# Fixing the issue order by hand in a recurrent-attention and feed-forward kernel

## The chip, the cores and the metric

The kernel runs on one core of a Trainium2 chip. The metric is the device time of one execution in microseconds (us). Before the change three runs had a median of 198.59 us (197.66 to 199.28). The profile adds one traced execution of each kernel; its span, from the first to the last instruction, was 195.0 us before. The profiled run itself was timed at 196.82 us, so a timed figure is about 2 us above a span.

The engines are called by the profile's names: PE is the tensor engine (PEld its weight loads), DVE is VectorE, ACT is ScalarE, POOL is GpSimd and SP issues most DMAs. Each engine has its own stream of instructions.

## The reference, cut to what matters

```python
# B, H, S, D = 4, 8, 768, 48
for t in range(S):
    state = alpha[:, :, t, :, None] * state + einsum('bhd,bhde...', k_t, v_t)   # outer product
    y[:, :, t] = einsum('bhd,bhde->bhe', q_t, state)
x = y.transpose(0, 2, 1, 3).reshape(3072, 384)
h = maximum(maximum(x @ w1, x @ w2), x @ w3)      # 384 -> 768
return (h @ w_out).astype(float32)                # 768 -> 384
```

The kernel cuts the sequence into blocks of 128 positions and takes two batches together. That gives 12 *steps* (6 blocks x 2 pairs of batches). A step goes through these pieces:

- **decays** (`N`, `D`): logarithm of alpha, cumulative sums by a triangular product, two exponentials; then q and k are scaled (the "q product" and the "k product"), and v by a constant (`V`);
- **turn** (`T`): q and k are transposed on PE, DVE copies them to `qkT`;
- **scores** (`A`): eight products per batch on 48 rows each, of heads at rows 0 to 47 and heads at rows 64 to 111, then a mask on DVE;
- **attention** (`Y`) and **turn back** (`X`), which gives `xT`;
- **state** (`S`): the state for the next block;
- **gates** (`G0` to `G8`): x against w1, w2, w3. Three groups of products per third of the weights; ACT copies two of them, DVE takes two maxima and writes `hT`;
- **output** (`O`): `hT` against `w_out`, an ACT copy and a store.

A gate group is 6 products of 256 columns; a step has 9 groups.

## The kernel before

The scheduler of the programming layer decides each engine's order. The kernel gives it whole stages:

```python
def cast_weights():                       # the casts are shared by three engines
    for e, dst, src in wstage:
        (nc.scalar.copy, nc.vector.tensor_copy, nc.gpsimd.tensor_copy)[e](out=dst, in_=src)   # shortened

# stage_a, per batch u: decays
lps = ps.tile([P, 512], FP32, name="lps", tag="w", bufs=2)
...
nc.gpsimd.tensor_mul(kv, rk[:, hs], ic)
nc.vector.tensor_mul(qv, rq[:, hs], ac)
...
nc.gpsimd.tensor_scalar_mul(vt, raws.pop((s, "v")), vs_c)

# stage_b: turn, scores, attention, turn back
for p in range(HP):
    for i in range(2):
        rows = slice(64 * i, 64 * i + D)
        nc.tensor.matmul(aps[i][:, p, :], qkT[rows, u, 1, p, :], qkT[rows, u, 0, p, :], ...)
...
nc.scalar.copy(out=xT..., in_=xtp)

# ffn, per third of the weights
nc.scalar.copy(out=h0, in_=gs[0])
nc.scalar.copy(out=h1, in_=gs[1])
nc.vector.tensor_max(h0, h0, h1)          # two fp16 inputs in SBUF
nc.vector.tensor_max(hs, gs[2], h0)

load(1); load_weights(); load(2); load(3)      # after load(0)
stage_a(0); stage_b(0); stage_a(1); cast_weights()       # shortened
for s in range(NS):
    load(s + 4); stage_b(s + 1); stage_a(s + 2); stage_c(s); ffn(s)     # with bounds
```

The kernel keeps eight buffers in PSUM, which holds PE's results, in three rings (a ring is a set of buffers used in turn): the ring `w` (2 buffers: decays, turns, scores), the ring `s` (2: attention, turn back, state, output) and the ring `g` (4: gates).

## Time and profile before

| what | value | view |
|---|---|---|
| span | 195.0 us | page |
| PE busy in 0:10, 40:50, 130:140 | 1.64, 7.02, 9.98 us | table by stretches |
| mean length of five late steps | 13.95 us, (168.68 - 98.93) / 5 | output products in the timeline |
| one gate group, late | 0.66 us | chain of waits |
| first gate products | 23.3 us | timeline |

The table by stretches gives, for each window, the busy time and the instruction count of each engine, the clock granted to PE, and the mean share and rate of the DMA engines. (PEclk is 1.00 also where the trace has no record of the clock: here the first record lies at 27.3 us, so the first two windows say nothing on it.) These are four windows of the kernel before:

```profile
core 0: us, PE busy (x) PEld busy (x) DVE busy (x) ACT busy (x) POOL busy (x), PEclk, DMA share, GB/s
0.00:10.00 10.00, 1.64 (x17) 1.31 (x18) 2.98 (x10) 4.25 (x8) 2.17 (x6) 1.00 1.05 186
10.00:20.00 10.00, 7.33 (x68) 4.88 (x66) 5.45 (x8) 5.44 (x11) 4.46 (x4) 1.00 1.28 256
40.00:50.00 10.00, 7.02 (x57) 4.46 (x55) 4.88 (x10) 4.93 (x12) 4.55 (x5) 0.83 1.19 213
130.00:140.00 10.00, 9.98 (x122) 7.52 (x120) 6.18 (x11) 6.74 (x15) 4.83 (x5) 1.00 1.00 197
```

PE starts slowly, has a hole in 40:50, and is busy almost all of the time late on. The timeline (start, duration, engine, line, operation, names, shapes, count) of a late step shows how the scheduler mixed half-row scores (line 193) into the gates (line 252):

```profile
158.32 0.49 PE L252 MATMUL gps_2615<-xT,wcat 128*128 128x256 f16 x3
158.83 0.39 PE L193 MATMUL aps_2504<-qkT 48*128 48x128 f16 x4
...
159.21 0.49 PE L252 MATMUL gps_2615<-xT,wcat 128*128 128x256 f16 x3
159.63 0.40 PE L193 MATMUL aps_2505<-qkT 48*128 48x128 f16 x4
```

The scores come four at a time, all four on the same rows, with full-height products (those that use all 128 rows of PE's array) between one four and the next. The duration of a group includes the pipeline's end, so starts are what to count with: 3 gate products from 158.32 take 3 x 0.109 = 0.33 us, to 158.65, and the scores only start at 158.83.

### The profile page before, as it was taken

The page shows a single profiled execution, that of the slowest core. Times are in us where ns is not written, and L with a number is a line of the kernel's source. Part 1 is how long each engine was busy: PE and PEld are TensorE (multiplying, and loading weights), DVE is VectorE, ACT ScalarE, POOL GpSimd, SP SyncE. Part 2 cuts the span into 40 slices and gives each one's busy share as a digit, 9 for nine tenths or more (in the row PEclk, how much of TensorE's full clock was granted, in tenths as well). Part 3 has the DMA queues.
Part 4 walks back from the last instruction along what each step waited for, and adds up shares of the span by engine and source line. Part 5 has one row for each costly group of instructions (what it writes and reads, how often), then busy time and mean ns, then how long its engine had stood idle before and what let it go on. Part 6 is the DMA issues. An engine that isn't in the chain of part 4 may idle for free.

```text
span 195.0 us, 4340 instructions
## 1 busy us (share of the span) xinstructions
PE 167.9 (86%) x1736; PEld 122.5 (63%) x1736; DVE 116.8 (60%) x200; ACT 110.7 (57%) x221; POOL 61.2 (31%) x64
## 2 busy tenths in 40 slices
PE   0295886958869979999989999999989999999992
PEld 0164564845556857766767857857757767778680
DVE  3272845526746996448468568667477666765250
ACT  2518066682552946753954956847827639446551
POOL 0443722054180646800540631703922304100000
PEclk9999999996999988999999999999999999999999
DMA  7999999999996059379699909819720020020102
GB/s 147 223 218 284 351 357 224 225 198 228 239 190 135 0 147 228 78 158 202 167 232 217 194 29 221 166 68 225 116 75 9 3 81 3 0 81 3 74 9 81
DMA packets 107252, 28.69 MB, mean 147 GB/s; under 512 B 99808, under 2 KB 107232, under 8 KB 107232
## 3 DMA queue, kind: packets, MB, share of 16 engines
q1 hardware_dynamic: 106944, 28.32, 67.5%
q8 instruction: 13, 0.21, 0.5%
q10 hardware_dynamic: 288, 0.10, 0.2%
q14 instruction: 7, 0.06, 0.1%
HBM read 23.69 MB, written 4.72 MB: 146 GB/s over the span
## 4 chain that ended last, share of the span: by engine, by line
PE 41%; DVE 16%; ACT 13%; issue 9%; POOL 9%; DMA 5%; SPq 4%; POOLq 0%; DVEq 0%; ACTq 0%
PE ops L267 7%; DVE hT L263 5%; PE tps L179 5%; ACT ic L157 4%; DMA rq<-in_q_dram 3%; SPq L85 3%; DMA ra<-in_alpha_dram 2%; ACT xb L208 2%; POOL vt L167 2%; POOL qk_86 L163 2%; ACT ac L158 2%; PE yps L204 2%; POOL gt L221 1%; DVE qkT L182 1%; PE xtp L210 1%
## 5 line engine op out<-in xcount | busy, mean ns | idle before, releaser
L252 PEld LDWEIGHTS <-wcat 128*128 128x128 f16 x648 | 58.0, 98 | 12.2 <-ACT wcat L131 1.9
L267 PE MATMUL ops<-wo_97,hT 128*128 128x384 f16 x144 | 29.2, 342 | 6.1 <-DVE hT L263 2.9
L167 POOL TENSOR_SCALAR vt<-rv,c_69 128x768 f16<-128x768 f32 x12 | 27.2, 2267 | 1.8 <-DMA rv<-in_v_dram 1.8
L267 PEld LDWEIGHTS <-hT 128*128 128x128 f16 x144 | 13.5, 102 | 18.2 <-DVE hT L263 7.6
L182 DVE COPY qkT<-tps 128x1024 f16<-128x1024 f16 x24 | 15.6, 686 | 14.9 <-PE tps L179 14.9
L208 ACT ACTIVATE xb<-yps,c_69 128x384 f16<-128x384 f32 x24 | 14.0, 583 | 17.7 <-PE yps L204 17.4
L270 ACT COPY ob<-ops 128x384 f32<-128x384 f32 x24 | 11.1, 488 | 20.2 <-PE ops L267 18.0
L193 PEld LDWEIGHTS <-qkT 48*128 48x128 f16 x192 | 11.7, 100 | 9.8 <-DVE qkT L182 4.3
L204 PE MATMUL yps<-vt,lat 128*128 128x48 f16 x192 | 14.9, 189 | 0.5 <-DVE lat L196 0.2
L163 POOL TENSOR_TENSOR qk_86<-rk,ic 128x384 f16<-128x384 f32 x6 | 6.0, 997 | 28.6 <-ACT ic L157 28.6
L157 ACT ACTIVATE ic<-lps,c_69 128x384 f32<-128x384 f32 x24 | 14.0, 584 | 1.3 <-PE lps L151 1.1
L163 POOL TENSOR_TENSOR qk_87<-rk,ic 128x384 f16<-128x384 f32 x6 | 6.0, 997 | 26.6 <-ACT ic L157 26.6
L158 ACT ACTIVATE ac<-lps,c_69 128x384 f32<-128x384 f32 x24 | 14.0, 584 | 0.0
L204 PEld LDWEIGHTS <-lat 128*128 128x128 f16 x192 | 11.5, 100 | 3.3 <-DVE lat L196 1.9
L163 POOL TENSOR_TENSOR qk_84<-rk,ic 128x384 f16<-128x384 f32 x6 | 6.2, 1039 | 21.2 <-ACT ic L157 21.2
L163 POOL TENSOR_TENSOR qk_85<-rk,ic 128x384 f16<-128x384 f32 x6 | 6.3, 1042 | 17.3 <-ACT ic L157 17.3
L211 ACT COPY xT<-xtp 128x768 f16<-128x768 f16 x12 | 9.6, 797 | 0.6 <-PE xtp L210 0.4
L210 PE MATMUL xtp<-c_68,xb 128*128 128x128 f16 x72 | 8.8, 236 | 1.0 <-ACT ge L159 0.5
L164 DVE TENSOR_TENSOR qk_84<-rq,ac 128x384 f16<-128x384 f32 x6 | 4.8, 808 | 7.5 <-DMA rq<-in_q_dram 6.0
L201 PEld LDWEIGHTS <-qkT 128*128 128x128 f16 x80 | 7.6, 97 | 0.7
L210 PEld LDWEIGHTS <-xb 128*128 128x128 f16 x72 | 4.5, 103 | 5.7 <-ACT xb L208 5.4
L164 DVE TENSOR_TENSOR qk_85<-rq,ac 128x384 f16<-128x384 f32 x6 | 4.6, 766 | 4.9 <-ACT ac L158 4.9
(436 smaller groups left out, 372.4 us busy)
## 6 DMA issues: line engine op xcount, KB each, us to landing
ra<-in_alpha_dram SPq DMA_DIRECT2D x12, 384.0 KB, 4.9
rk<-in_k_dram SPq DMA_DIRECT2D x12, 384.0 KB, 6.2
rq<-in_q_dram SPq DMA_DIRECT2D x12, 384.0 KB, 5.7
rv<-in_v_dram SPq DMA_DIRECT2D x12, 384.0 KB, 5.5
out_dram<-ob SPq DMA_DIRECT2D x24, 192.0 KB, 2.0
ws_0_106<-in_moe_w_dram SPq DMA_DIRECT2D x1, 384.0 KB, 5.1
ws_1_108<-in_moe_w_dram SPq DMA_DIRECT2D x1, 384.0 KB, 4.5
ws_2_110<-in_moe_w_dram SPq DMA_DIRECT2D x1, 384.0 KB, 5.1
```

Of the source, the lines that this page charges most:

```text
L157: nc.scalar.activation(out=ic, in_=lv, func=AFT.Exp, bias=nat_c, scale=-1.0)
L158: nc.scalar.activation(out=ac, in_=lv, func=AFT.Exp, bias=at_c, scale=1.0)
L163: nc.gpsimd.tensor_mul(kv, rk[:, hs], ic)
L167: nc.gpsimd.tensor_scalar_mul(vt, raws.pop((s, "v")), vs_c)
L182: nc.vector.tensor_copy(out=qkT[:, u], in_=tps)
L193: nc.tensor.matmul(aps[i][:, p, :], qkT[rows, u, 1, p, :], qkT[rows, u, 0, p, :], start=True, stop=True)
L204: nc.tensor.matmul(yps[:, p, i, :], la_[:, i, p, :], vt[:, u * H + 2 * p + i, :], start=(cb == 0), stop=(cb == 0 or i == 1))
L208: nc.scalar.mul(xb, yps.rearrange("p a b d -> p (a b d)"), ys_c)
L210: nc.tensor.transpose(xtp[:, u, f, :], xb[:, f * P:(f + 1) * P], ident)
L252: nc.tensor.matmul(gps[:, j, :], wcat[:, f, g, jj * P:(jj + 1) * P], xT[:, f].rearrange("p u t -> p (u t)"), start=(f == 0), stop=(f == NF ...
L267: nc.tensor.matmul(ops, hT[:, jj, u * P:(u + 1) * P], wo16[:, jj, :], start=(jj == 0), stop=(jj == NJ - 1))
L270: nc.scalar.copy(out=ob, in_=ops)
```

## The change

Its intent: take the order out of the scheduler's hands, do the attention of three steps before the first gates so that the wait for weights is filled, let each arriving third of the weights serve two steps, and keep PE's clock up early with products whose result is not used. Work also moves between engines. The core of the diff (helper functions that only became separate pieces are cut):

```diff
-    def cast_weights():                     # three engines
+    def cast_weights(_, i):
+        for dst, src in wstage[3 * i:3 * i + 3]:
+            nc.gpsimd.tensor_copy(out=dst, in_=src)
 ...
-            nc.gpsimd.tensor_mul(kv, rk[:, hs], ic)
-            nc.vector.tensor_mul(qv, rq[:, hs], ac)
+        eng = nc.vector if s < 3 else nc.gpsimd
+        nc.gpsimd.tensor_mul(kv, raws[s, "k"][:, hs], ic)
+        eng.tensor_mul(qv, raws[s, "q"][:, hs], ac)
 ...
-        nc.gpsimd.tensor_scalar_mul(vt, raws.pop((s, "v")), vs_c)
+        nc.scalar.mul(vt, raws.pop((s, "v")), vs_c)
 ...
-        nc.scalar.copy(out=xT.rearrange("p f u t -> p u f t"), in_=xtp)
+            nc.vector.tensor_copy(out=xT.rearrange("p f u t -> p u f t"), in_=xtp_of.pop(s))
 ...
+    def warm(_, n):
+        wps = ps.tile([P, 512], FP32, name="wps", tag="g", bufs=4)
+        for _ in range(n):
+            nc.tensor.matmul(wps, blank[:, :P], blank, start=True, stop=True)
 ...
+    # letter = piece, digit = batch, gate group or count, @n = step; without @ the loop's step plus an offset
+    PROLOGUE = """N0@0 H11@0 D0@0 D1@0 N0@1 H8@0 V0@0 T0@0 T1@0 A0@0 A1@0 D0@1 Y0@0 D1@1 X0@0 Y1@0
+        T0@1 H2@0 A0@1 T1@1 N0@2 V0@1 A1@1 X1@0 Y0@1 D0@2 D1@2 X0@1 H5@0 T0@2 Y1@1 M0@0 T1@2
+        S0@0 V0@2 A0@2 S1@0 W0 X1@1 A1@2 W1 W2 W3"""
+    FIRST = """G0@0 G1@0 G2@0 G0@1 G1@1 G2@1 Y0@2 G3@0 G4@0 G5@0 G3@1 G4@1 Y1@2 X0@2 G5@1 G6@0 G7@0
+        G8@0 G6@1 X1@2 G7@1 G8@1"""
+    SECOND = """N0@3 G0 G1 G2 D0@3 D1@3 M0@1 G3 G4 O0@0 G5 T0 O1@0 G6 N0 S0 O0@1 A0 V0@3 G7 T1 D0 S1
+        O1@1 A1 G8 Y0 Y1 D1 M0 X0 V0 X1"""
+    STEADY = """T0 S0 N0 G0 G1 D0 T1 S1 O1 A0 G2 G3 O0 A1 G4 Y0 G5 Y1 X0 G6 D1 X1 G7 V0 G8 M0"""
+    LAST = """G0 G1 G2 G3 G4 G5 O0 G6 G7 G8 O1"""
     load(1)
+    load(2)
     load_weights()
-    load(2)
     load(3)
+    load(4)
 ...
+    with tc.manual_schedule():
+        emit(0, PROLOGUE); emit(0, FIRST)                   # joined here
+        for s in range(2, NS):
+            emit(s, {2: SECOND, NS - 1: LAST}.get(s, STEADY))
```

`M` computes the state's gates; `T`, `A`, `Y`, `X` without `@` mean the next step, `N`, `D`, `V` the one after it, `O` and `S` the one before.

## The prediction

> **What bounds the kernel now.** The profiled span is 195.0 us (timed median 198.59). The table by stretches shows three regimes.
>
> - 0 to 30 us is start-up: the tensor engine is busy 1.6, 7.3 and 8.9 of each 10 us, and products run at half speed: 16 transposes took 1.90 us (0.89 later), six gate products 1.29 us (0.66 later). Full speed comes at 34 us.
> - 30 to 80 us has holes: busy 7.0 in 40:50, 8.0 in 50:60. At 44.4 us, after 2.6 us idle, twelve output products took 3.7 us instead of 1.98.
> - From 80 us the tensor engine is busy 9.4 to 10 of 10 us (one dip, 8.8); a step takes 13.6 to 14.4 us (output products at 142.2, 156.6, 170.2 us in the chain of waits).
>
> Start-to-start times of a late step, from the timeline: gates 54 x 0.1094 = 5.91, output 1.98, transposes in 0.90, scores 16 x 0.082 = 1.31, attention 0.70, transposes back 0.36, decays 0.54, state 0.66: 12.36 us. So about 1.2 us a step are short waits (hT, qkT, xb) and switches.
>
> **What changes.** Product counts stay, but for 26 idle products early (off the path). On ACT, xT copies (0.80) leave and v scaling comes (estimate 0.85): 9.9 us per step. Vector loses q products from step 3 and gains xT: 9.3. GpSimd loses the 2.2 us v scaling and gains two 1.0 us products: 4.6. None reaches 12.3. All casts go to GpSimd: 12 x 0.83 us, and weights land every 1.15 us.
>
> Step 2's loads move ahead of the weights: 1.57 MB at the measured 0.22 MB/us delays weights by 7.1 us, to 25.6 us for the first, groups complete about 28, 31.6, 35.8, output 39. The three attention steps end near 26 us, so this wait is filled, and two steps per group (3.9 us of products against 3.5 us of loading) make the tensor engine the limit.
>
> **Sum.** Gates of step 0 start about 26.5 us. The first two steps' gates (FIRST) are 12.9 us of products, plus 2 us for landings and slow products: 41.5. SECOND: 14.9 us, ends 56.5. Eight steady steps at 12.3: 155. LAST and output 9.9, then copy and store (3.3 us at the chain's end): 168.
>
> One gain is hard to size: scores now alternate rows 0 and 64. The Trainium skill, "TensorE: Matmul & The Clock Gate", Part 3, says weight loads overlap running products only where row groups differ; before, four on the same rows came every 82 ns. If they pair, 0.3 to 0.7 us a step. Against it I set 0.4 us of waits a step, since a fixed order cannot slip past a late operand. Net span 167, timed 170.
>
> **What would show it right.** First gate products at 25 to 28 us; FIRST done by 40 to 43; no tensor idle over 1.5 us and no slow output products (310 ns) after 45 us; steady period 12.0 to 12.7, busy over 9.5 in every stretch; scores closer than 82 ns; weights landing 7 us later, with no loss.
>
> **What would make it wrong.** Two PSUM buffers per ring, or ACT's order (80% busy), stalling every steady step: each 0.3 us costs 3 us. The tensor engine going slow between 20 and 30 us (the same page, Part 1, says some 3.4 us of idleness halve the clock; this trace agrees after start and at 44 us). Scores pairing fully: 4 us better. Step 3's loads, now last, landing at 46 us while SECOND wants its transposes at 47.
>
> Time 170 us, range 164 to 177. Chances: faster by over 2% 0.97, within 2% 0.02, slower 0.01.

## The result, and the profile after

The changed kernel took 176.37 us (median of four runs, one of them slow) against 198.67 us for the kernel before. The ratio is 0.8873, with a 95% interval of 0.8824 to 0.8923. Here and below, a ratio is the mean time of one kernel's fast runs over the mean of the other's fast runs of the same rounds, so it is not quite the ratio of the quoted medians. The profiled span is 174.4 us.

The four windows, for the kernel after:

```profile
core 0: us, PE busy (x) PEld busy (x) DVE busy (x) ACT busy (x) POOL busy (x), PEclk, DMA share, GB/s
0.00:10.00 10.00, 7.95 (x38) 3.31 (x39) 3.22 (x11) 4.20 (x7) 2.16 (x6) 1.00 1.03 182
10.00:20.00 10.00, 6.26 (x74) 4.02 (x72) 6.69 (x10) 5.32 (x10) 1.99 (x2) 0.68 1.38 219
...
40.00:50.00 10.00, 9.92 (x96) 8.38 (x95) 4.82 (x10) 7.67 (x16) 4.15 (x5) 1.00 0.93 180
...
130.00:140.00 10.00, 9.22 (x123) 7.68 (x122) 7.04 (x12) 8.27 (x16) 3.07 (x5) 1.00 0.08 27
```

The hole in 40:50 is closed. In 130:140, though, PE is busy *less* than before (9.22 against 9.98) and still gets more done, because a step needs fewer busy microseconds. Four steady steps measured from one output to the next each show 12.04 us of PE busy time in 12.82 us; the five late steps before had 67.09 us of busy time in 69.75, so 13.42 in 13.95 each.

The scores explain most of that (f2 below). In the timeline of the kernel after (tiles `aps_872` are on rows 0 to 47, `aps_873` on rows 64 to 111):

```profile
52.14 1.14 PE L282 MATMUL ops<-wo_97,hT 128*128 128x384 f16 x6
53.21 0.23 PE L193 MATMUL aps_872<-qkT 48*128 48x128 f16 x1
53.21 0.23 PE L193 MATMUL aps_873<-qkT 48*128 48x128 f16 x1
53.27 0.22 PE L193 MATMUL aps_872<-qkT 48*128 48x128 f16 x1
53.28 0.22 PE L193 MATMUL aps_873<-qkT 48*128 48x128 f16 x1
```

Two scores start within 0.01 us of each other, and the next pair 0.06 us later. The page "TensorE: Matmul & The Clock Gate" of the Trainium skill describes this in Part 3: products on different row groups run at the same time in the array. This trace agrees, in that the starts differ by 0.01 us or less.

Where the 20.6 us of the span came from, by milestones in the two timelines:

| milestone | before | after | gain so far |
|---|---|---|---|
| first output product of step 2 | 74.9 | 63.0 | 11.9 |
| first output product of step 9 | 168.7 | 152.4 | 16.3 |
| first output product of step 11 | 189.2 | 168.7 | 20.5 |

The milestones have not done quite the same work: the new order is further ahead with attention, which is why its last step has only gates and outputs left and gains another 4 us there. (The 168.7 is the start of the seventh of the last 18 output products, which begin at 167.76 us; the first six belong to step 10.)

What did *not* go to plan is visible too. The gates start at 31.34 us, and the granted clock was 0.68 in 10:20. And every steady step has one hole on PE. The timelines of DVE, POOL and PE around it, in this order:

```profile
97.93 1.27 DVE L275 TENSOR_TENSOR h_1698<-h_1698,h_1730 128x512 f16<-128x512 f16 x1 [1.03 <-ACT h_1730 L273]
99.30 0.69 DVE L276 TENSOR_TENSOR hT<-gps_1734,h_1698 128x512 f16<-128x512 f32 x1
99.91 0.68 DVE L183 COPY qkT<-tps 128x1024 f16<-128x1024 f16 x1
```

```profile
96.95 1.00 POOL L159 TENSOR_TENSOR qk_87<-rk,ic 128x384 f16<-128x384 f32 x1 [6.84 <-ACT ic L155]
97.91 1.01 POOL L160 TENSOR_TENSOR qk_87<-rq,ac 128x384 f16<-128x384 f32 x1
```

```profile
97.45 0.61 PE L179 MATMUL tps<-c_68,qk_87 128*128 128x128 f16 x8
...
99.54 0.33 PE L146 MATMUL lps<-la_80,c_68 128*128 128x384 f16 x1
100.64 0.61 PE L179 MATMUL tps<-c_68,qk_87 128*128 128x128 f16 x8 [0.78 <-DVE qkT L183]
```

The maximum at line 275 takes 0.42 us elsewhere in the same step (at 104.13 and at 107.08 us). Here it takes 1.27 us, beside POOL's q product at 97.91 us, which the change had moved to POOL. The page "SBUF — State Buffer" of the Trainium skill, section "Who interferes with whom", says that a DVE instruction with two SBUF inputs contends with a GpSimd instruction that reads SBUF, and that one of them blocks. The trace fits: POOL's q product runs until 98.92 us and the maximum ends 0.28 us after it. It is not any POOL instruction, though: in the kernel before, the maximum at 98.66 us took 0.41 us in the middle of POOL's scaling of v (from 97.67 us), and of the eleven maxima and q products that ran on DVE wholly beside that scaling nine took their usual time. So the change took a neighbour off POOL that mostly did not disturb DVE, and put one there that does. The copy to `qkT` stands behind the maximum in DVE's order, the ring `w` has only two buffers, and so the second turn waits 0.78 us.

### The profile page after: what moved, and what is told of

Its sections match the earlier page's. It is cut to its first block, busy times and chain, and to the rows that moved or that the text cites. A ratio compares the mean times of both kernels' runs of the same rounds, so it can differ in the third digit from the quotient of the medians.

```text
span 174.4 us, 4372 instructions
## 1 busy us (share of the span) xinstructions
PE 156.9 (90%) x1762; PEld 120.2 (69%) x1762; DVE 116.1 (67%) x191; ACT 108.4 (62%) x205; POOL 57.1 (33%) x78
## 4 chain that ended last, share of the span: by engine, by line
PE 78%; DVE 10%; ACT 4%; DMA 3%; issue 2%; SPq 1%; ACTq 0%; DVEq 0%
PE ops L282 14%; PE tps L179 6%; DVE qkT L183 4%; DVE lat L196 4%; DMA rq<-in_q_dram 3%; PE yps L210 2%; PE lps L146 2%; PE xtp L222 2%; PE yps L207 2%; PE wps L293 2%; PE sps L250 2%; PE sps L247 1%; SPq L85 1%; ACT xb L214 1%; PE lps L149 1%
## 5 line engine op out<-in xcount | busy, mean ns | idle before, releaser
L268 PEld LDWEIGHTS <-wcat 128*128 128x128 f16 x648 | 59.8, 98 | 8.7 <-issue 0.3
L282 PE MATMUL ops<-wo_97,hT 128*128 128x384 f16 x144 | 27.0, 326 | 0.6 <-DVE st_1_93 L254 0.6
L282 PEld LDWEIGHTS <-hT 128*128 128x128 f16 x144 | 13.6, 98 | 7.5 <-issue 0.7
L183 DVE COPY qkT<-tps 128x1024 f16<-128x1024 f16 x24 | 16.3, 686 | 2.6 <-PE tps L179 2.5
L193 PEld LDWEIGHTS <-qkT 48*128 48x128 f16 x192 | 6.1, 97 | 11.0 <-issue 7.5
L210 PE MATMUL yps<-vt,lat 128*128 128x48 f16 x192 | 11.8, 188 | 0.1
L170 ACT ACTIVATE vt<-rv,c_69 128x768 f16<-128x768 f32 x12 | 11.5, 957 | 0.0
L225 DVE COPY xT<-xtp 128x768 f16<-128x768 f16 x12 | 6.7, 556 | 7.0 <-PE xtp L222 7.0
L293 PE MATMUL wps<-blank 128*128 128x512 f16 x26 | 10.2, 553 | 1.2 <-DVE blank L340 1.2
L210 PEld LDWEIGHTS <-lat 128*128 128x128 f16 x192 | 10.2, 100 | 0.7 <-DVE lat L196 0.3
L293 PEld LDWEIGHTS <-blank 128*128 128x128 f16 x26 | 3.1, 130 | 5.2 <-issue 3.3
L179 PE MATMUL tps<-c_68,qk_85 128*128 128x128 f16 x48 | 4.5, 248 | 2.3 <-DVE qkT L183 1.6
```

The source lines that it names most:

```text
L179: nc.tensor.transpose(tps[:, i, p, :], qk[:, i, u * HP + p].rearrange("p a b -> p (a b)"), ident)
L183: nc.vector.tensor_copy(out=qkT, in_=tps)
L210: nc.tensor.matmul(yps[:, p, i, :], lat[:, i, p, :], vt[:, u * H + 2 * p + i, :], start=(cb == 0), stop=(cb == 0 or i == 1))
L268: nc.tensor.matmul(gps[:, j, :], wcat[:, f, g, jj * P:(jj + 1) * P], xT[:, f].rearrange("p u t -> p (u t)"), start=(f == 0), stop=(f == NF ...
L282: nc.tensor.matmul(ops, hT_of[s][:, jj, u * P:(u + 1) * P], wo16[:, jj, :], start=(jj == 0), stop=(jj == NJ - 1))
L293: nc.tensor.matmul(wps, blank[:, :P], blank, start=True, stop=True)
```

## The experiments

Twelve kernels ran. The e runs start from the changed kernel, as does f3. f1, f2, f2c, f4, g1 and g2 start from e4, and h1 from g2. Each was run with the kernel before on the same chip.

| run | median us | ratio to before | 95% interval | span us |
|---|---|---|---|---|
| the change | 176.37 | 0.8873 | 0.8824 to 0.8923 | 174.4 |
| e1_q_on_vector | 187.67 | 0.9480 | 0.9407 to 0.9554 | 186.8 |
| e2_scores_by_half | 175.91 | 0.8900 | 0.8865 to 0.8935 | 173.4 |
| e3_no_idle | 179.96 | 0.9093 | 0.9054 to 0.9132 | 177.9 |
| e4_max_after_turn | 169.64 | 0.8587 | 0.8555 to 0.8619 | 167.7 |
| f1_two_ahead (wrong result) | 180.49 | 0.9154 | 0.9076 to 0.9231 | 177.7 |
| f2_scores_apart | 180.79 | 0.9140 | 0.9076 to 0.9204 | 180.2 |
| f2c_scores_together | 173.93 | 0.8822 | 0.8757 to 0.8888 | 171.6 |
| f3_scheduler | 182.39 | 0.9221 | 0.9172 to 0.9271 | 180.7 |
| f4_one_step_at_a_time | 171.41 | 0.8652 | 0.8593 to 0.8711 | 169.9 |
| g1_two_ahead_mended | 177.57 | 0.9035 | 0.8992 to 0.9078 | 175.6 |
| g2_scores_in_gate_banks | 168.44 | 0.8560 | 0.8529 to 0.8590 | 166.4 |
| h1_no_late_idle | 167.72 | 0.8467 | 0.8393 to 0.8542 | 166.6 |

One of the four runs of the change and one of f2c were slow; the medians of their fast runs are 176.26 and 173.46 us. The differences in microseconds below are between medians of different rounds. The ratios put e4's gain at 5.7 us instead of 6.7 and e3's loss at 4.4 instead of 3.6, so they are good to about 1 us.

### The hole in the steady step: e4 and e1

**e4_max_after_turn** changes DVE's order alone. The last pair of maxima of a step is issued after the copy of the next step's first turn. PE, ACT and POOL keep their orders.

```diff
+        elif jg == 2 and 3 <= s < NS - 1:
+            held[s] = (gps, h_of[0], h_of[1])      # the two maxima are issued later, by piece Z
-    STEADY = """T0 S0 N0 G0 ...
+    STEADY = """T0 Z0 S0 N0 G0 ...
```

> Only the order on VectorE changes: the last maximum of a step is issued after the copy of the next step's first turn, so a collision with GpSimd can no longer hold that copy. Theory A (the 0.78 us wait per steady step is the maximum held by the GpSimd q product and the copy queued behind it): the wait goes, steady period 12.8 to about 12.1 us, 4 to 6 us faster. Theory B (the turn waits for its PSUM buffer for another reason, such as the decays' copy on ACT): period stays within 0.2 us of 12.8.

It was 6.7 us faster (169.64 against 176.37). DVE's timeline in e4:

```profile
95.78 0.69 DVE L183 COPY qkT<-tps 128x1024 f16<-128x1024 f16 x1 [1.20 <-PE tps L179]
96.39 0.50 DVE L285 TENSOR_TENSOR h<-h,h 128x512 f16<-128x512 f16 x1
96.92 0.69 DVE L286 TENSOR_TENSOR hT<-gps,h 128x512 f16<-128x512 f32 x1
98.03 0.69 DVE L183 COPY qkT<-tps 128x1024 f16<-128x1024 f16 x1
```

The copy goes first, the maximum starts when POOL's q product (95.59 to 96.60 us) is nearly done and takes 0.50 us, and PE has no gap left. The window is one steady step of e4, from output to output:

```profile
core 0: us, PE busy (x) PEld busy (x) DVE busy (x) ACT busy (x) POOL busy (x), PEclk, DMA share, GB/s
86.28:98.16 11.88, 11.88 (x152) 9.64 (x150) 8.65 (x16) 8.77 (x18) 4.48 (x6) 1.00 0.95 194
```

The period fell from 12.82 to 11.88 us, all of it busy. Theory A holds (it expected about 12.1 us), and the gain in period (0.94 us) is somewhat more than the 0.78 us that the profile charged to the wait.

**e1_q_on_vector** asks whether the q product should have stayed on DVE.

```diff
-        eng = nc.vector if s < 3 else nc.gpsimd
+        eng = nc.vector
```

> The q products stay on VectorE in all steps (undoes the move to GpSimd). In the changed kernel the last maximum of each steady step (two fp16 inputs in SBUF) took 1.27 us instead of 0.42 beside the GpSimd q product, and the second turn of the next step then waited 0.78 us. Theory A (that collision costs the wait): no 1.27 us maxima, wait for qkT falls to 0.2 us or less, 2 to 5 us faster in all, less the 1.1 to 2 us of work per step that VectorE gets back. Theory B (VectorE is simply full and in order): the wait stays or grows, time the same or up to 4 us slower.

It was 11.3 us slower, which is worse than both theories allowed. The collision was gone from the maxima of the steady steps (they took 0.41 to 0.43 us). But now the q product stands at the head of DVE's queue and waits for ACT. Its timeline in e1:

```profile
105.24 0.99 DVE L160 TENSOR_TENSOR qk<-rq,ac 128x384 f16<-128x384 f32 x1 [1.90 <-ACT ac L156]
106.15 0.55 DVE L225 COPY xT<-xtp 128x768 f16<-128x768 f16 x1
```

The copies behind it arrive late, and PE waits for `xT` and for `qkT` in each step; the period became 13.97 us. DVE was not full (10.3 us busy in 13.97), so theory B names the right place but for a wrong reason: not the amount of work, but an operand that comes late at the head of a queue. And the collision was not gone, only moved: each q product of the steady steps took 0.98 to 0.99 us on DVE, beside POOL's k product (here 104.81 to 105.81 us), where q products that met no POOL product took 0.55 (the change, at 9.37 us). That is about 0.4 us twice a step, on top of the waits for ACT; no run separates the two. So in this order moving the q product to POOL was right even with its collision, and the order was what needed mending. The order had been made for POOL, so e1 says nothing on the best order with q on DVE.

### The scores: e2, f2 and f2c

**e2_scores_by_half** issues four scores on the first rows and then four on the second, instead of alternating.

```diff
-        for p in range(HP):
-            for i in range(2):
+        for i in range(2):
+            for p in range(HP):
```

> Scores issued four on rows 0 to 47, then four on rows 64 to 111, as the scheduler had them before. Theory A (alternating halves pair in the array): groups of eight go from 0.33 us back to about 0.66, so 0.65 us a step, 9 steps after the start, 5 to 7 us slower. Theory B (the scores' gain is hidden by waits, so only slack is lost): under 2 us slower.

Nothing changed (ratio 0.890, against 0.887 for the change). It would be wrong to read this as that the scores do not matter. PE's timeline in e2:

```profile
100.34 1.14 PE L282 MATMUL ops<-wo,hT 128*128 128x384 f16 x6
101.42 0.41 PE L193 MATMUL aps<-qkT 48*128 48x128 f16 x8
101.75 1.48 PE L268 MATMUL gps<-xT,wcat 128*128 128x256 f16 x12
```

The eight products still start in pairs (101.415 and 101.429 us, then 101.482 and 101.495, and so on) and take 0.33 us together: PE overlaps a four on one half with a four on the other when they are next to each other. The semaphores show which is which: the second to start carries the wait of the second four, and the signals of both fours are on the last two. So the fifth product of the stream started before the second. My edit had not undone the thing in dispute. The alternation that the prediction pointed at is not what matters; being adjacent is.

**f2_scores_apart** puts a gate group between the two fours, as the scheduler had done before. **f2c_scores_together** has the same shifted order of the attention, but with the fours next to each other.

```diff
-    STEADY (e4)  ... S1 O1 A0 G2 G3 O0 A1 G4 Y0 G5 Y1 X0 G6 ...
+    STEADY (f2)  ... S1 O1 B0 G2 C0 G3 O0 B1 G4 C1 G5 Y0 Y1 X0 G6 ...
+    STEADY (f2c) ... S1 O1 B0 C0 G2 G3 O0 B1 C1 G4 G5 Y0 Y1 X0 G6 ...     # B, C: the two halves of A
```

> On e4: in every steady step a gate group stands between the four scores on rows 0 and the four on rows 64. e2 showed that 4+4 back to back overlap as well as alternating ones, so it did not undo the pairing. Theory A (the scores gain because two row halves stand next to each other and run at once): each step costs 0.7 to 1.0 us more on the tensor engine, 8 steps, 5 to 8 us slower than e4. Theory B (the halves do not matter): within 1.5 us of e4.

> Control for f2: the same late order of attention and turn back as in f2, but with the two halves of the scores next to each other again. f2 was 11 us slower than e4 (180.8 against 169.6). Theory A (0.86 us a step of it is the separated halves, as group starts in f2 show: four scores cost 0.43 us, eight cost 0.44 us): 6 to 8 us faster than f2, 172 to 175 us. Theory B (the reordered attention causes it): within 2 us of f2.

f2 took 180.79 us, 11.2 us more than e4 and beyond theory A's 5 to 8, and f2c 173.93. So 6.9 us (6.3 by the ratios) lie in the separation alone, and some 4 us of f2's loss over e4 are the shifted order (its turn back waits for ACT, about 0.3 us a step). The groups show the cost directly. PE in f2, then in e4:

```profile
105.48 0.83 PE L271 MATMUL gps<-xT,wcat 128*128 128x256 f16 x6
106.24 0.39 PE L199 MATMUL aps<-qkT 48*128 48x128 f16 x4
106.57 0.83 PE L271 MATMUL gps<-xT,wcat 128*128 128x256 f16 x6
```

```profile
98.16 1.14 PE L292 MATMUL ops<-wo,hT 128*128 128x384 f16 x6
99.23 0.40 PE L193 MATMUL aps<-qkT 48*128 48x128 f16 x8
99.56 1.48 PE L268 MATMUL gps<-xT,wcat 128*128 128x256 f16 x12
```

In f2, six gates from 105.48 end their issue at 106.13 (6 x 0.109), and the next gate starts at 106.57: four scores cost 0.44 us. In e4, six outputs from 98.16 end at 99.13 (6 x 0.1625), and the next gate starts at 99.56: eight scores cost 0.43 us. So the second four is free if it is adjacent. Only half of the 0.44 us is the scores themselves: within a four they start 0.055 us apart, and the rest is at the two changes between gates and scores (0.21 us from the last gate's start to the first score in f2, 0.14 us from the last score to the next gate, where a gate follows a gate after 0.109 us). A step has four such fours, so putting them together saves 4 x 0.44 less 2 x 0.43, or 0.9 us a step. The measured periods agree: 13.21 us in f2 against 12.37 us in f2c, a difference of 0.84.

### The idle products: e3 and h1

**e3_no_idle** drops all 26 of them.

```diff
         for piece in order.split():
+            if piece[0] == 'H':
+                continue
```

> The 26 idle products are left out. In the changed kernel the clock was halved from about 14 to 26 us in spite of them, and two groups (0.85 and 2.13 us) lie on the chain of waits. Theory A (they only delay): the first gate product starts 0.5 to 2.5 us earlier than 31.3 us and the time falls by as much. Theory B (they keep the clock up where it matters): the gates begin at half speed, first gate groups take 1.3 us, 1 to 3 us slower.

It was 3.6 us slower. Products up to 37 us then ran at half speed. The first 16 transposes, in e3 and in the change:

```profile
9.60 1.89 PE L179 MATMUL tps<-c,qk 128*128 128x128 f16 x16 [2.61 <-DVE qk L160]
```

```profile
9.50 1.09 PE L179 MATMUL tps<-c_68,qk_84 128*128 128x128 f16 x16 [0.86 <-DVE qk_84 L160]
```

The gates, which started at 32.92 us instead of 31.34, were issued every 0.21 us for about twenty products before they reached 0.11. Theory B holds for the outcome, a little beyond its 1 to 3 us. The line of the granted clock is no help in e3: it shows 9 from the first slice, but e3's trace has no record of the clock before 37.0 us, and the line shows 9 where there is none. These are the lines of the two pages, 40 slices of the span each, e3 first:

```profile
PEclk9999999999999999999999999999999999999998
```

And the changed kernel:

```profile
PEclk9995558999999999999999999999999999999999
```

The drop in the second is on record: after the early idle products PE waits often, and from 13.6 to 27.3 us the granted clock is 0.5. The page "TensorE: Matmul & The Clock Gate", Part 1, gives about 3.4 us of idleness as enough for that. Here less was enough: in the 3.4 us before the drop PE was busy for 1.58 us, with no gap over 0.9 us, and in the kernel before the clock fell at 44.3 us after only 2.5 us without work on PE. Where the limit lies these runs do not show.

**h1_no_late_idle** (on g2, below) drops only the six late idle products and keeps the nineteen at the start.

```diff
-    ... T0@1 T1@1 H2@0 X1@0 ... Y1@1 H4@0 M0@0 T0@2 ...
+    ... T0@1 T1@1 X1@0 ... Y1@1 M0@0 T0@2 ...
```

> g2 without its six late idle products (two at 18.7 us, four at 24.2 us); the nineteen before 10 us stay. Without any (e3) the first six gate groups ran mostly at half speed. Theory A (the late ones are the ones that count: they bring the clock up just before the gates): transposes of step 2 and the first gate groups at half speed, gates start up to 1 us later or at the same time, 1 to 3 us slower than g2 (168.4 us). Theory B (they only lie in the way, the early ones or the real products suffice): gates start 0.5 to 1 us earlier, 0 to 1 us faster.

The gates started at 28.41 us instead of 29.75 (theory B), but the first twelve gate products were slow (twelve of them 1.83 us, where e4 has 1.48 later; theory A; the clock rose at 29.2 us). The two effects cancel within the noise: 167.72 us against 168.44, with overlapping intervals. So the late idle products neither help nor hurt measurably. That would leave e3's 3.6 us to the early ones, but e3 and h1 have different starts around them, and no run dropped the early ones alone. By which route they could still help at 28 us, when the clock has long fallen again, these runs do not show.

### The start: f1, g1, f4 and g2

**f1_two_ahead** and **g1_two_ahead_mended** load the weights before step 2, as the kernel before did, start the gates after two steps of attention, and put the attention of step 2 later.

```diff
     load(1)
-    load(2)
     load_weights()
+    load(2)
-    PROLOGUE = """... steps 0 to 2 ..."""
+    PROLOGUE = """... steps 0 and 1 ..."""
+    FIRST (g1) = """... G8@0 N0@2 D0@2 O0@0 D1@2 O1@0 M0@0 G6@1 G7@1 T0@2 S0@0 G8@1 T1@2 V0@2 A0@2 S1@0
+        O0@1 A1@2 O1@1 Y0@2 Y1@2 X0@2 X1@2"""
```

> On e4 (169.6 us): attention only two steps ahead of the weights. Weights are loaded before step 2, the gates of steps 0 and 1 may start at about 25 us instead of 31, the attention of step 2 and the outputs of steps 0 and 1 fill the end of that stage. Theory A (three steps ahead costs start-up time, since it delays the weights by 7 us and the gates by about as much): the second stage ends 2 to 4 us earlier than 59 us, total 2 to 4 us faster. Theory B (three ahead pays, since step 2 loaded last lands at about 39 us and its serial chain then leaves the tensor engine idle): 0 to 3 us slower.

f1's result was wrong (relative error 0.108). Two gate groups of different steps used the same buffer entry in the emission code. Its time is not used further. g1 mends that and spreads the outputs better:

> f1 with its mistake mended (two gate groups shared a buffer name, so it was wrong) and with the outputs of steps 0 and 1 and three held-back gate groups placed into the wait for step 2. Theory A (two ahead is better once well ordered): first turn of step 4 at 55 to 58 us against 59.2 in e4, 166 to 168 us. Theory B (three ahead pays, since step 2's loads end at 39 us and its chain of about 10 us runs with too little to fill it): first turn of step 4 at 60 us or later, 170 to 176 us.

g1 took 177.57 us, 7.9 us more than e4. Its gates started at 24.76 us, 6 us earlier than in e4, but its first turn of step 4 came at 67.32 us instead of 59.15. Step 2's attention ends at about 53 us with too little other work around it, and step 3's then follows in the same way. Theory B holds, with a loss beyond its range of 170 to 176 us: three steps ahead pays against this order. My order was written once and not tuned, so part of the 8 us may be the order.

**f4_one_step_at_a_time** (on e4) does nine gate groups of step 0 and then nine of step 1.

```diff
-    FIRST = """G0@0 G1@0 G2@0 G0@1 G1@1 G2@1 Y0@2 G3@0 G4@0 G5@0 G3@1 ...
+    FIRST = """G0@0 G1@0 G2@0 G3@0 G4@0 G5@0 Y0@2 G6@0 G7@0 G8@0 G0@1 G1@1 ...
```

> On e4: nine gate groups of step 0, then nine of step 1, instead of both steps per weight group. Theory A (a weight group must feed two steps, or the tensor engine waits for loads): it waits about 2 us for the third group (GpSimd cast its last part at 37.9 us), 1.5 to 2.5 us slower than e4. Theory B (the late start at 31 us has left enough weights in hand): within 0.7 us.

It was 1.8 us slower by the medians (171.41 against 169.64); the two intervals overlap slightly. The trace supports theory A. PE waits three times for a cast, 1.5 us in all. From the waits of f4 between 30 and 50 us (who waited for whom: us in total, times, longest):

```profile
PE gps L268 <- POOL wcat L130: 1.5, 3, 0.9
```

**g2_scores_in_gate_banks** (on e4) lets the scores of the first three steps use the four gate buffers, idle at that time. It also reorders the start (decays and turns come earlier) and has one idle product less; these lines are not shown.

```diff
+        ring = dict(tag="g", bufs=4) if s < 3 else dict(tag="w", bufs=2)
-        aps = [ps.tile([P, HP, P], FP32, name=f"aps{i}", tag="w", bufs=2) for i in range(2)]
+        aps = [ps.tile([P, HP, P], FP32, name=f"aps{i}", **ring) for i in range(2)]
```

> On e4: in the first three steps the scores use the four PSUM buffers of the gates, which are idle then, instead of the ring of two that turns and decays use, and the order of the start is adapted. Theory A (the start is a chain through the ring of two, so gates begin at 31 us although the first cast weights are ready at 28.7): first gate product at 28 to 29.5 us, 1 to 2.5 us faster than e4. Theory B (the loads of step 2 bound the start): within 0.7 us of e4.

The gates started at 29.75 us (just outside theory A's 28 to 29.5) instead of 30.93, and the medians differ by 1.2 us (168.44 against 169.64), but the two kernels ran in different rounds and the intervals of their ratios overlap. The ring of two and the order around it were part of the chain at the start, together some 1.2 us of it; g2 does not separate them. With h1, this is the fastest version found, at 0.847 to 0.856 of the time before; between g2 and h1 the runs do not decide.

### The order alone: f3

**f3_scheduler** keeps the pieces, their emission order, the moved work and the idle products of the change, but lets the scheduler fix each engine's order.

```diff
-    with tc.manual_schedule():
+    with ExitStack():
```

> The changed kernel's pieces in the same emission order, but the scheduler again decides each engine's order. Theory A (the hand-fixed order is what brings the gain): 184 to 197 us. Theory B (the work moved and the emission order bring it, and the scheduler keeps most of it): 172 to 182 us.

It took 182.39 us, just outside both ranges. By the ratios, f3 takes 7.8% off the kernel before, the change 11.3% and e4 14.1%. So most of the change's gain came with the restructured pieces and only part with the hand-fixed order. Of the 6.3 us between the spans, 4.4 lie before the first output product of step 2 (67.4 us against 63.0), and f3's clock rose only at 36.9 us where that of the change rose at 27.3; in the later steps f3 needs 12.96 us each and the change 12.78. In f3's timeline around 95 us, for instance, the scores stand eight together too. Mending the order (e4) was worth about as much as fixing it.

## Why the prediction was right or wrong

The predicted 170 us (164 to 177) holds the measured 176.37, near its upper end. The spans show the terms: 167 predicted, 174.4 measured.

- **"Gates of step 0 start about 26.5 us": 31.3.** This was the largest miss, 4.8 us. The loads were reckoned at a steady 0.22 MB/us, giving 25.6 us for the first weights. They landed at 27.4 us (issued at 22.19, 5.2 us to landing); 1.2 us of that lateness is one issue by SP that took 2.99 us instead of about 1.75, while the queue ran almost dry. But that was not what bound: the first weights were cast by 28.7 us. The step that failed was "the three attention steps end near 26 us": the last scores of step 2 started at 31.2 us, right before the gates, at the end of a chain that ran at half clock from 13.6 to 27.3 us (named as a risk for 20 to 30 us), with the ring of two and the order around it worth some 1.2 us (g2). In h1, with a shorter chain, the gates started at 28.41 us.
- **"FIRST 12.9 us of products, plus 2 us": 12.9 us, from 31.3 to 44.3.** The products were counted right, and the allowance was not needed, since by 31 us the weights were there and the clock was up. SECOND ended near 59.6 us where the prediction had 56.5, so 3.1 us of the miss survived.
- **"12.36 us a step" and "0.4 us of waits a step".** The miss is in the second term. The products of a step need 11.88 us (e4), which is what the predicted 12.3 leaves without its 0.4 of waits. The waits were 0.94 us a step (12.82 less 11.88). Putting the scores together saved 0.84 us a step and not 0.3 to 0.7 (f2 against f2c), but about 0.4 of that are changes between gates and scores, which the 12.36 did not count. The net was 12.82 against 12.3 in a steady step, some 3 us over the eight steps after SECOND. Of the things that would make the prediction wrong, "two PSUM buffers per ring" was named and was where the wait showed, but its cause was not seen: a DVE maximum held by the very product that the change moved to POOL (e4).
- **"Scores closer than 82 ns … alternate rows".** The gain is real, the reason only half right. 82 ns was 0.33 us over four, with the change to other products included; within a four they start some 0.06 us apart. What counts is that fours on different rows stand next to each other (e2, f2).
- **"26 idle products early (off the path)".** Not quite: 2.13 us of them lay on the chain of waits at 25.3 us and 0.85 at 18.2 us. Without any the kernel was 3.6 us slower (e3), and without the late ones there was no difference (h1).
- **"A fixed order cannot slip past a late operand".** Right, and shown most clearly by e1, where one late operand at the head of DVE's queue, and a collision of the same product, cost 11 us.
- **"Two steps per group … make the tensor engine the limit".** f4's trace supports it: about 1.5 us of waits without it.
- **"Weights landing 7 us later, with no loss".** The delay was 8.9 us (18.5 before, 27.4 after). Not delaying them cost more in the one order tried (g1).

That the range held is in part luck: the unused allowance took back about 2 of the 4.8 us at the start, and only that left room for a steady wait whose cause had not been foreseen.

## What to carry to other kernels

When work moves to an idle engine, check two things: whether it now shares a memory port with an instruction of another engine, and what stands behind that instruction in its queue. In this kernel the collision lost less than a microsecond a step, and placing one copy ahead of it won all of that back. Put products on different halves of the array next to each other, in any order, and keep full-height products from between them. And when an experiment shows no effect, look in its trace whether the edit undid the thing in dispute before reading anything into the time.

## What the Trainium skill lacked or had wrong

- "TensorE: Matmul & The Clock Gate", Part 3, says that products start in program order. In e2, by the semaphores, the fifth of eight (on other rows) started 0.014 us after the first, and the second only 0.067 us after it. So the overlap of row groups needs no alternation: four products on one half followed by four on the other took the same 0.33 us as alternating ones. The page does not say what a group of half-height products between full-height ones costs: 0.44 us for four, 0.43 us for eight.
- The same part says that weight loads overlap running products only where row groups differ. In steady steps the full-height gate products start every 0.109 us although each has its own weight load of 0.098 us on the same rows, so those are overlapped here; the page's own remark about a background weight buffer fits better.
- Part 1 of that page warns that the clock events of a trace can be unreliable, but no page that I read says that there may be none before the first change of the clock: in e3 the first is at 37.0 us, and the profile's line shows 9 until the last slice, while 16 early transposes took 1.89 us and 8 of them later 0.61.
- "SBUF — State Buffer", section "Who interferes with whom", fits for POOL's products and casts: a maximum with two fp16 inputs in SBUF took 1.27 us instead of 0.42 beside a product, and 1.09 beside a cast (the change, 35.44 us). Its rule is wider than the trace: beside POOL's scaling of v, which reads SBUF too, nine of eleven DVE instructions with two SBUF inputs took their usual time. It does not mention that the larger loss is in what queues behind it: a copy that stood behind cost PE 0.94 us a step.
- No page that I read explains the dip of the DMA queue near 20 us: with loads still to be issued, the rate fell from 220 to 17 GB/s for about a microsecond while SP spent 2.99 us on one issue instead of about 1.75. Most variants show the same; e3, without idle products, does not at this place. Its cause stays open.
